# One attention kernel with expert layers: the sync queue's order written out, a half-size layout for the keys, and two stores of row sums instead of twelve

## The chip, the cores and the metric

The kernel runs on one core of one Trainium2 chip. The metric is device time in microseconds (us) from launch to end, the median of several runs. Engines are named as the profile names them: PE is the matrix engine, DVE the vector engine, ACT the scalar engine, POOL the GpSimd engine, and SP the sync engine, which here only issues transfers (DMAs). An engine works through its own instructions strictly in order; a DMA that SP issues must wait on SP for whatever its buffer or its source still needs, and everything behind it on SP waits too.

## The reference, cut to what matters

```python
# q, k, v: (8, 8, 576, 64), float32; batch B, heads H, positions S, width D
scores = scale * np.matmul(q, k.transpose(0, 1, 3, 2))
x = (psi_rel / psi_i)[..., None]              # from the positions alone
bias = np.maximum(x @ w1 + b1, 0.0) @ w2      # (S, S, H): one table per head
scores = scores + bias.transpose(2, 0, 1)[None]
attn = np.exp(scores - np.max(scores, axis=-1, keepdims=True))
attn = attn / (np.sum(attn, axis=-1, keepdims=True) + 1e-09)
out = np.matmul(attn, v)
x = out.transpose(0, 2, 1, 3).reshape(B * S, H * D)   # 4608 tokens x 512
return ((x @ moe_w1) * (x @ moe_w2) @ moe_w3) @ moe_w_out
```

The expert layers' weights arrive as 64-bit floats, which the kernel reads as pairs of 32-bit words and turns into 32-bit floats itself. The keys and queries come transposed, positions along the free dimension.

## The kernel before

**Three stages.** First a prologue computes the bias tables of all eight heads in 36 groups (`bias_group`): DVE and ACT make the hidden layer, PE multiplies, ACT scales the result into a tile `bev` (four buffers), and SP stores it to a table in device memory, `nb_d`. Then the attention runs, and last the expert layers in nine chunks of 512 tokens, three matmul passes to each product (lines 605 to 649), which read the attention's result from device memory and multiply it with the reciprocal row sums (`load_x`, `load_r`).

**Units.** The attention is worked through in 32 units, u = 0 to 31: four pairs of heads p, and in each the eight batches b. A unit has nine tiles of 128 rows: "0", "2", "4", "6" are head 0, "1", "3", "5", "7" head 1, and "M" the last 64 rows of both. For each tile PE multiplies queries with keys (`op_S`, line 259), DVE adds the bias and finds the row extreme (`op_T`, line 270, tile `ts`), ACT takes the exponential and, in the same instruction, the row sum (`op_E`, line 299), and DVE transposes pairs of tiles in 32 x 32 blocks (`op_R`, line 309, tile `pt`). One unit later PE multiplies the transposed block with v (`op_W`, line 352, eight parts W0 to W7), ACT copies the result out (`op_X`), and SP stores it (`op_x`, `x_d`). Every fourth unit DVE turns the collected sums into reciprocals (`op_r`, lines 316 to 319), and SP stores them to `r_m` and `r_t`.

**Transfers of a unit.** The steps l load q and k two units ahead, one tile per head (two buffers each, 288 KB a transfer), and v one unit ahead in four parts (one buffer each, 320 or 256 KB). `load_bias` loads the bias tables of a pair into two buffers per tile group: for pair 0 from the prologue's plan, for pair p + 1 from `op_T` in units b = 2 to 6 of pair p, one group a unit (576 KB, group M 288 KB). A queue of 24 weight pieces (`piece_of`, `narrow`) is converted beside the attention in units with b = 1 to 6: step c0 loads a piece's words (`wi`, 512 KB, two buffers), c1 and c2 are on ACT (lines 140 and 143; the first makes `wmag`), c3 and c7 on POOL (lines 146, 163, 164), c4 to c6 on DVE (lines 149, 155, 160).

**What sets the order.** `arrange` gives every step of every unit a planned time, in units of about a microsecond:

```python
PERIOD = 9 * L_T                                   # 12.87, a unit
at[f"lv{c}"] = -PERIOD + at[f"W{2 * c + 1}"][0] + 0.6, "SP"
at["c0"] = 0.2, "SP"
at["c1"] = t_of[1] + 1.6, "ACT"                    # 4.26
```

Worked out modulo the period, SP's steps stand at 0.2 (c0), 1.40 (v, last part), 2.50 (`op_x`), 4.50 (row sums), 6.36 and 6.46 (k and q of head 0, first part of v), 9.32 (v, second part), 11.31 and 11.41 (k and q of head 1, third part of v). The first tile's T stands at 2.00. `drive` sorts a plan by these times and emits the steps one by one. Inside `manual_schedule` the engines that are named keep the emitted order. SP is not among them: the order of its DMAs comes from the compiler's list scheduler, which lets a transfer go when, by its own estimate, buffer and data are ready. The plan is driven in several parts: steps at times below zero with the prologue, then the attention (line 506), then the fold and the expert layers. 

Of the kernel before, what the change touches and what calls it, by code (L numbers as in the profile page):

```python
# [9 lines left out]
F32 = mybir.dt.float32  # L10
# [8 lines left out]
P = 128  # L19
# [59 lines left out]
def relpos_attention_moe(  # L79
# [17 lines left out]
    nc = tc.nc  # L97
    NPAIR, B, _, S2 = q.shape
    S, D, H = S2 // 2, P // 2, 2 * NPAIR
# [5 lines left out]
    HS = S // 2  # L105
# [7 lines left out]
    dram = ctx.enter_context(tc.tile_pool(name="dram", bufs=1, space=DRAM))  # L113
# [52 lines left out]
        steps = [fetch, size, rest, clamp, shift, head, power, total]  # L166
        return steps if WIDE else [fetch] + [lambda: None] * 7

    def drive(plan):

        E_ = mybir.EngineType
        with tc.manual_schedule(engines={E_.PE, E_.Activation, E_.DVE, E_.Pool}):
            for _, _, step in sorted(plan, key=lambda e: e[:2]):
                step()

# [15 lines left out]
    nb_d = dram.tile([H, (S + 1) * NB_W], F32, name="nb_d")  # L191
    nb_v = nb_d[:, 0:S * NB_W].rearrange("h (i w) -> h i w", w=NB_W)[:, :, NB_L:NB_L + S]
    x_d = [dram.tile([P, NTOK], F32, name=f"x_d{p}") for p in range(NPAIR)]
    r_m = [dram.tile([2, B * 512], F32, name=f"r_m{p}") for p in range(NPAIR)]
    r_t = [dram.tile([2, B * 64], F32, name=f"r_t{p}") for p in range(NPAIR)]

# [1 line left out]
    raw = att_r.enter_context(tc.tile_pool(name="raw", bufs=2, side="right"))  # L200
# [6 lines left out]
    st = {u: {} for u in range(NU)}  # L207
# [27 lines left out]
    def op_l(u, which):  # L235
        p, b = units[u]
        n = int(which[1])
        if which[0] == "v":
            b0, b1 = VB[n]
            t = vp.tile([P, b1 - b0, 2, D], F32, name=f"v{n}")  # L240
            src = v[p, b].rearrange("p (b h d) -> p b h d", h=2, d=D)[:, b0:b1]
            for i in range(b0, b1):
                st[u]["v", i] = t[:, i - b0]
        else:
            t = st[u][which] = raw.tile([P, S], F32, name=which)
            src = {"q": q, "k": k}[which[0]][p, b][:, n * S:(n + 1) * S]
        nc.sync.dma_start(t, src)

    def op_S(u, t):

        d = st[u]
        s = d["s", t] = ps_s.tile([P, 2, 512], F32, name="s")
        for hf, rows in enumerate((lo, hi)):
            for g, outs in enumerate((lo, hi)):
                if t == "M":
                    h, q0 = g, 512
                else:
                    h, q0 = int(t) % 2, int(t) // 2 * P + 64 * g
                nc.tensor.matmul(  # L259
                    s[outs, hf, :HS], d[f"q{h}"][rows, q0:q0 + 64],  # L260
                    d[f"k{h}"][rows, hf * HS:(hf + 1) * HS], start=True, stop=True,
                )

    def op_T(u, t):
# [16 lines left out]
    for i in range(2):  # L281
        t = att.enter_context(tc.tile_pool(name=f"sums{i}", bufs=1)).tile([P, 64], F32, name=f"sums{i}")
# [28 lines left out]
    def op_r(u, n):  # L311
        if u % 4 < 3:
            return
        if n == "":
            r = SUMS[u // 4 % 2]
            nc.vector.tensor_scalar(r[:, 0:36], r[:, 0:36], 1e-9, None, op0=ALU.add)
            nc.vector.reciprocal(r[:, 0:36], r[:, 0:36])
            st[u]["rt"] = sm.tile([P, 64], F32, name="rt")
            nc.vector.transpose(st[u]["rt"], r)
            return  # L320
        p, b = units[u]
        rt, b0 = st[u]["rt"], b - 3
        for a in range(4):
            for h in range(2):
                o = r_m[p][h, b0 * 512:(b + 1) * 512].rearrange("(n a j) -> a n j", a=4, j=32)[a]
                nc.sync.dma_start(o, rt[32 * a + 16 * h:32 * a + 16 * h + 16, 0:32])
            o = r_t[p][a // 2, b0 * 64:(b + 1) * 64].rearrange("(b g j) -> g b j", g=2, j=32)[a % 2]
            nc.sync.dma_start(o, rt[32 * a:32 * a + 4, 32:64])

    def load_r(rb, p, rows, h, t0, t1):  # L330
        n = t0
        while n < t1:
            b, j = divmod(n, S)
            e = min(t1, b * S + (512 if j < 512 else S))
            src = r_m[p][h:h + 1, b * 512 + j:b * 512 + j + e - n] if j < 512 else \
                r_t[p][h:h + 1, b * 64 + j - 512:b * 64 + j - 512 + e - n]
            nc.sync.dma_start(rb[rows, n - t0:e - t0], src.broadcast_to([64, e - n]))
            n = e

    def op_W(u, n):  # L340
# [44 lines left out]
    def op_c(u, n):  # L385
        pieces[u][int(n)]()

    made = dict(l=op_l, S=op_S, T=op_T, E=op_E, R=op_R, r=op_r, W=op_W, X=op_X, x=op_x, c=op_c)
    later = []
    for (n, u), (at, on) in arrange(NU, pieces).items():  # L390
        step = lambda n=n, u=u: made[n[0]](u, n[1:])
        later.append((at, len(later), step, n, u))
    t_s = max(e[0] for e in later if e[3][0] in "SE") + 0.5
    end = max(e[0] for e in later) + 0.5
    later = [e[:3] for e in later]

    plan = [e for e in later if e[0] < 0.0]
    later = [e for e in later if e[0] >= 0.0]


    with ExitStack() as pro:
# [29 lines left out]
        def reach(G):  # L431

            return (G + 1) * GR - 1, S - 1 - G * GR
# [9 lines left out]
        for G in range(NGRP):  # L443
            n = max(reach(G)) + 1
            for vv in range(GV):
                e = min(busy, key=lambda e: busy[e] + COST[e][0] + COST[e][1] * n)
# [40 lines left out]
        for G in range(NGRP):  # L487
            at = -LEAD + G * PACE_B
            put(plan, bias_group(G), *(at + d for d in AT_BIAS))
            for ts in GROUPS:  # L490
                if G == (NGRP - 1 if ts == "M" else 8 * (int(ts[-1]) // 2) + 7):
                    plan.append((at + AT_BIAS[-1] + LAG_B, len(plan), lambda ts=ts: load_bias(0, ts)))
        drive(plan)


# [7 lines left out]

    PT = [pt.tile([P, 9, S], F32, name=f"pt{i}") for i in range(2)]

    drive([e for e in later if e[0] < t_s])
    later = [e for e in later if e[0] >= t_s]
    att_r.close()

# [74 lines left out]
    def load_x(c):  # L584
        for cc in range(NC):
            xr = xs.tile([P, CH], F32, name=f"xr{cc}", bufs=1)
            nc.sync.dma_start(xr, x_d[cc][:, c * CH:(c + 1) * CH])
            rb = xs.tile([P, CH], F32, name=f"rb{cc}", bufs=1)
            for h, rows in enumerate((lo, hi)):
                load_r(rb, cc, rows, h, c * CH, (c + 1) * CH)  # L590
            chunks[c]["x"][cc] = (xr, rb)
        yield
# [64 lines left out]
    for t in range(2):  # L657
        for m in range(2):
            put_w(later, w01, t, m, t_s + AT_W1 + PACE_W * (2 * t + m))
    drive([e for e in later if e[0] <= end])  # L660
    later = [e for e in later if e[0] > end]
    att.close()
# [3 lines left out]
    plan, t_f = [], t_s + AT_F + N_F * PACE_F0 + (2 * NF - N_F) * PACE_F + AT_FOLD[3]  # L666
# [77 lines left out]
```

## Time and profile before

| what | value |
|---|---|
| runs | 1175.22, 1181.52, 1184.53 us; median 1181.52 |
| profiled execution | 1180.03 us, its span 1178.2 us |
| PE / DVE / ACT / POOL busy | 1112.6 / 686.3 / 484.1 / 181.2 us |
| attention, first ts at | 65.7 us |
| expert layers' first `up` matmul on the chain at | 585.1 us |
| granted PE clock | 0.98 over the span |
| DMA traffic | 158.5 MB; share of the 16 engines 71% from 72 to 517 us, 13% after 700 us |

The profile's page gives busy time and shares for each engine, then groups of instructions: line, engine, operation, output<-input, count, then busy us, mean ns of one, and the idle time before them with what ended most of it. "issue" is idle time that ended though no semaphore was waited for. Rows of single instructions begin with the start and the duration in us; in brackets stand the idle time before and its releaser. The chain of waits is the path that ended last, followed back through whatever released each step. A row of a table by stretches gives the stretch, its length, the busy time of PE, PE's weight loads, DVE, ACT and POOL, the granted clock, the DMA share and GB/s. A row by DMA queue gives packets, MB and the share of 16 engines; q1 carries the kernel's data.

### The profile page before, as it was taken

The page shows a single profiled execution, that of the slowest core. Times are in us where ns is not written, and L with a number is a line of the kernel's source. Part 1 is how long each engine was busy: PE and PEld are TensorE (multiplying, and loading weights), DVE is VectorE, ACT ScalarE, POOL GpSimd, SP SyncE. Part 2 cuts the span into 40 slices and gives each one's busy share as a digit, 9 for nine tenths or more (in the row PEclk, how much of TensorE's full clock was granted, in tenths as well). Part 3 has the DMA queues.
Part 4 walks back from the last instruction along what each step waited for, and adds up shares of the span by engine and source line. Part 5 has one row for each costly group of instructions (what it writes and reads, how often), then busy time and mean ns, then how long its engine had stood idle before and what let it go on. Part 6 is the DMA issues. An engine that isn't in the chain of part 4 may idle for free.

```text
span 1178.2 us, 34156 instructions
## 1 busy us (share of the span) xinstructions
PE 1112.6 (94%) x14720; PEld 771.2 (65%) x14720; DVE 686.3 (58%) x1284; ACT 484.1 (41%) x1071; POOL 181.2 (15%) x152
## 2 busy tenths in 40 slices
PE   7769989998899999898999999999999999999998
PEld 3225445444444554466888888888888888888887
DVE  8779988998899999986885222223131222223111
ACT  6756655665566666664442212121211212121212
POOL 0003320321033123333543000000000000000000
PEclk9979999999999999998999999999999999999999
DMA  8887786767776766636431211202010211100000
GB/s 261 279 261 229 231 285 206 242 214 244 234 234 222 237 222 205 217 120 173 132 117 54 72 36 54 54 36 72 35 55 19 72 36 56 52 36 1 36 1 36
DMA packets 91959, 158.51 MB, mean 135 GB/s; under 512 B 18336, under 2 KB 32800, under 8 KB 91808
## 3 DMA queue, kind: packets, MB, share of 16 engines
q1 hardware_dynamic: 91376, 156.31, 41.6%
q8 instruction: 115, 1.88, 0.6%
q14 instruction: 36, 0.29, 0.1%
q10 hardware_dynamic: 432, 0.02, 0.0%
HBM read 126.36 MB, written 29.92 MB: 133 GB/s over the span
## 4 chain that ended last, share of the span: by engine, by line
PE 68%; DVE 19%; issue 5%; DMA 5%; ACT 2%; SPq 0%; DVEq 0%; POOL 0%; ACTq 0%; POOLq 0%
PE up L614 33%; PE o L639 17%; PE acc L352 8%; DVE ts L270 8%; DVE pt L309 7%; PE s L259 6%; PE wacc L573 3%; DMA nb_d<-bev 2%; DMA v<-in_v_dram 1%; PE bacc L473 1%; DVE wmag L155 1%; ACT pp L299 1%; DVE wi L160 1%; DVE zdve L459 1%; PE w3t L561 0%
## 5 line engine op out<-in xcount | busy, mean ns | idle before, releaser
L352 PE MATMUL acc<-pt,v 32*64 32x128 f32 (+1 forms) x9216 | 245.0, 298 | 21.9 <-issue 12.2
L352 PEld LDWEIGHTS acc<-pt,v 32*64 32x64 f32 x9216 | 158.2, 133 | 145.0 <-issue 110.7
L622 DVE TENSOR_TENSOR g<-up,a 128x512 f32<-128x512 f32 x72 | 49.8, 691 | 342.8 <-PE up L614 342.8
L299 ACT ACTIVATE pp<-ts,mx 128x576 f32<-128x576 f32 x256 | 196.5, 769 | 95.0 <-DVE mx L270 93.9
L259 PE MATMUL s<-k,q 64*64 64x288 f32 x2304 | 208.8, 442 | 21.2 <-DVE mx L270 16.0
L614 PE MATMUL up<-xl,wh 128*128 128x512 f32 x576 | 225.1, 391 | 0.0
L614 PE MATMUL up<-xh,wl 128*128 128x512 f32 x576 | 225.1, 391 | 0.0
L614 PE MATMUL up<-xh,wh 128*128 128x512 f32 x576 | 225.1, 391 | 0.0
L270 DVE CUSTOM_DVE_ANT_0 ts<-s,nb 128x576 f32<-128x576 f32 x256 | 184.9, 745 | 41.1 <-PE s L259 28.2
L639 PE MATMUL o<-w3s,gh 128*128 128x512 f32 x576 | 177.7, 390 | 0.0
L309 DVE STREAM_TRANSPOSE pt<-pp 128x1152 f32<-128x1152 f32 x128 | 175.5, 1371 | 0.1
L619 ACT COPY a<-up 128x512 f32<-128x512 f32 x72 | 42.3, 587 | 257.7 <-PE up L614 257.7
L259 PEld LDWEIGHTS s<-k,q 64*64 64x64 f32 x2304 | 63.3, 135 | 97.8 <-issue 48.1
L614 PEld LDWEIGHTS up<-xh,wl 128*128 128x128 f32 x576 | 108.2, 188 | 23.4
L614 PEld LDWEIGHTS up<-xl,wh 128*128 128x128 f32 x576 | 108.2, 188 | 23.4
L614 PEld LDWEIGHTS up<-xh,wh 128*128 128x128 f32 x576 | 108.2, 188 | 23.3
L639 PEld LDWEIGHTS o<-w3s,gh 128*128 128x128 f32 x576 | 108.1, 188 | 22.9
L625 ACT ACTIVATE gh<-g 128x512 fp32r<-128x512 f32 x72 | 45.5, 633 | 178.3 <-DVE g L622 178.3
L639 PE MATMUL o<-w3s,gl 128*128 128x512 f32 x288 | 112.1, 389 | 0.0
L600 POOL TENSOR_SCALAR xh<-xr 128x512 fp32r<-128x512 f32 x36 | 23.2, 645 | 443.3 <-DVE xr L596 443.3
L628 DVE TENSOR_TENSOR gl<-g,gh 128x512 fp32r<-128x512 f32 x72 | 51.6, 717 | 50.7 <-ACT gh L625 50.5
L146 POOL TENSOR_SCALAR wmag<-wmag 128x512 f32<-128x512 f32 x24 | 46.0, 1915 | 207.9 <-ACT wmag L140 174.0
(67 smaller groups left out, 937.3 us busy)
## 6 DMA issues: line engine op xcount, KB each, us to landing
v<-in_v_dram SPq DMA_DIRECT2D x64, 320.0 KB
k<-in_k_dram SPq DMA_DIRECT2D x64, 288.0 KB
q<-in_q_dram SPq DMA_DIRECT2D x64, 288.0 KB
v<-in_v_dram SPq DMA_DIRECT2D x64, 256.0 KB
wi<-in_moe_w_dram SPq DMA_DIRECT2D x32, 512.0 KB
nb_d<-bev SPq DMA_DIRECT2D x36, 295.5 KB
nb<-nb_d SPq DMA_DIRECT2D x16, 576.0 KB
x_d<-x SPq DMA_DIRECT2D x32, 288.0 KB
```

What stands on the lines that cost most here:

```text
L146: clamps.tensor_scalar(d["mag"], d["mag"], LEAST, MOST, op0=ALU.max, op1=ALU.min)
L259: nc.tensor.matmul(s[outs, hf, :HS], d[f"q{h}"][rows, q0:q0 + 64], d[f"k{h}"][rows, hf * HS:(hf + 1) * HS], start=True, stop=True,)
L270: nc.vector.tensor_tensor_reduce(out=halves(ts), in0=d.pop(("s", t))[:, :, :HS], in1=halves(NB[p, t]), op0=ALU.add, op1=ALU.min, scale=-1. ...
L299: nc.scalar.activation(d["p", ps][:, k * S:(k + 1) * S], ts, AF.Exp, bias=mx, scale=-1.0, accum_out=SUMS[u // 4 % 2][:, col:col + 1],)
L309: nc.vector.transpose(o, st[u].pop(("p", ts)))
L352: nc.tensor.matmul(acc[outs, a, c0:c0 + 32 * (t1 - t0)], d["v", b][rows, h], pt_[rows, t0:t1, 32 * b:32 * b + 32], start=(b == 0), stop=(b ...
L614: nc.tensor.matmul(acc, l[:, cc], r, start=(n == 0), stop=(n == 3 * NC - 1))
L619: nc.scalar.copy(a, ps[0])
L622: nc.vector.tensor_tensor(g, ps[1], a, op=ALU.mult)
L625: nc.scalar.activation(gh, g, AF.Copy)
L628: nc.vector.tensor_tensor(gl, g, f(gh), op=ALU.subtract)
L639: nc.tensor.matmul(d["o", t], l[:, sl], folded[ft][:, r], start=(ft == 0 and n == 0), stop=(ft == NF - 1 and n == 2),)
```

## The change

It has three parts.

1. SP joins the engines that keep the emitted order, in the attention's part of the plan only (line 506).
2. A key tile holds one head's 576 positions as 288 columns: positions 0 to 287 on partitions 0 to 63 and 288 to 575 on partitions 64 to 127. Before, both partition halves held all 576. The matmuls read the same rows; each transfer has 144 KB instead of 288. The host's layout of k follows.
3. The reciprocal row sums of four units go out in two transfers, one of [128, 32] to `r_m` and one of [128, 32] to `r_t`, instead of eight and four. Both destinations are laid out anew, and `load_r` reads `r_t` in two pieces of 32 positions.

```diff
-    def drive(plan):
+    def drive(plan, *more):
...
-        with tc.manual_schedule(engines={E_.PE, E_.Activation, E_.DVE, E_.Pool}):
+        with tc.manual_schedule(engines={E_.PE, E_.Activation, E_.DVE, E_.Pool, *more}):
...
-    r_m = [dram.tile([2, B * 512], F32, name=f"r_m{p}") for p in range(NPAIR)]
-    r_t = [dram.tile([2, B * 64], F32, name=f"r_t{p}") for p in range(NPAIR)]
+    r_m = [dram.tile([B // 4, 2, 4 * 512], F32, name=f"r_m{p}") for p in range(NPAIR)]
+    r_t = [dram.tile([B // 4, P, 32], F32, name=f"r_t{p}") for p in range(NPAIR)]
...
-            t = st[u][which] = raw.tile([P, S], F32, name=which)
-            src = {"q": q, "k": k}[which[0]][p, b][:, n * S:(n + 1) * S]
+            w = S if which[0] == "q" else HS
+            t = st[u][which] = raw.tile([P, w], F32, name=which)
+            src = {"q": q, "k": k}[which[0]][p, b][:, n * w:(n + 1) * w]
...
-                    d[f"k{h}"][rows, hf * HS:(hf + 1) * HS], start=True, stop=True,
+                    d[f"k{h}"][rows, :], start=True, stop=True,
...
-        rt, b0 = st[u]["rt"], b - 3
-        for a in range(4):
-            for h in range(2):
-                o = r_m[p][h, b0 * 512:(b + 1) * 512].rearrange("(n a j) -> a n j", a=4, j=32)[a]
-                nc.sync.dma_start(o, rt[32 * a + 16 * h:32 * a + 16 * h + 16, 0:32])
-            o = r_t[p][a // 2, b0 * 64:(b + 1) * 64].rearrange("(b g j) -> g b j", g=2, j=32)[a % 2]
-            nc.sync.dma_start(o, rt[32 * a:32 * a + 4, 32:64])
+        rt = st[u]["rt"]
+        o = r_m[p][b // 4].rearrange("h (n a j) -> a (h n) j", a=4, j=32)
+        nc.sync.dma_start(o, rt[:, 0:32])
+        nc.sync.dma_start(r_t[p][b // 4], rt[:, 32:64])
...
+                src = r_t[p][b // 4].rearrange("(h g b) j -> h b g j", h=2, g=2)[h:h + 1, b % 4].broadcast_to([64, 2, 32])
+                o = o.rearrange("p (g j) -> p g j", g=2)
...
-    drive([e for e in later if e[0] < t_s])
+    drive([e for e in later if e[0] < t_s], mybir.EngineType.SP)
```

More of the change, by code (lines that the diff above doesn't have):

```diff
@@ L334, in load_r @@
             e = min(t1, b * S + (512 if j < 512 else S))
-            src = r_m[p][h:h + 1, b * 512 + j:b * 512 + j + e - n] if j < 512 else \
-                r_t[p][h:h + 1, b * 64 + j - 512:b * 64 + j - 512 + e - n]
-            nc.sync.dma_start(rb[rows, n - t0:e - t0], src.broadcast_to([64, e - n]))
+            o = rb[rows, n - t0:e - t0]
+            if j < 512:
+                j += b % 4 * 512
+                src = r_m[p][b // 4, h:h + 1, j:j + e - n].broadcast_to([64, e - n])
+            else:
+                assert e - n == 64
+                src = r_t[p][b // 4].rearrange("(h g b) j -> h b g j", h=2, g=2)[h:h + 1, b % 4].broadcast_to([64, 2, 32])
+                o = o.rearrange("p (g j) -> p g j", g=2)
+            nc.sync.dma_start(o, src)
             n = e
@@ L712 @@
     pairs = heads // 2
-    for n in "qk":
-        a = inputs[n].reshape(-1, pairs, 2, seq, dim)
-        a = a.transpose(1, 0, 4, 2, 3)
-        inputs[n] = _np.concatenate([a, a], axis=2).reshape(pairs, -1, 2 * dim, 2 * seq)
+    a = inputs["q"].reshape(-1, pairs, 2, seq, dim).transpose(1, 0, 4, 2, 3)
+    inputs["q"] = _np.concatenate([a, a], axis=2).reshape(pairs, -1, 2 * dim, 2 * seq)
+    a = inputs["k"].reshape(-1, pairs, 2, 2, seq // 2, dim).transpose(1, 0, 3, 5, 2, 4)
+    inputs["k"] = a.reshape(pairs, -1, 2 * dim, seq)
     a = inputs["v"].reshape(-1, pairs, 2, seq // 32, 32, dim).transpose(1, 0, 4, 3, 2, 5)
```

## The prediction

> **What bounds the kernel now.** I read the page first, then the stretches of the attention stage, then the chain of waits, and last the queues and single instructions where the chain jumps.
>
> ```profile
> span 1178.2 us, 34156 instructions
> PE 1112.6 (94%) x14720; PEld 771.2 (65%) x14720; DVE 686.3 (58%) x1284; ACT 484.1 (41%) x1071; POOL 181.2 (15%) x152
> q8 instruction: 115, 1.88, 0.6%
> ...
> L352 PE MATMUL acc<-pt,v 32*64 32x128 f32 (+1 forms) x9216 | 245.0, 298 | 21.9 <-issue 12.2
> ```
> ```profile
> 159.46:192.69 33.23, 29.08 (x724) 15.07 (x720) 24.89 (x50) 16.59 (x42) 2.55 (x2) 0.90 0.72 229
> ...
> 278.38:310.47 32.09, 27.27 (x728) 14.45 (x728) 24.96 (x50) 16.59 (x42) 2.55 (x2) 0.95 0.82 258
> ```
>
> The busy 94% of PE is an average. After about 585 us the expert layers run on PE without a hole, and no edit touches PE work there. The attention stage (about 66 to 517 us, 32 units of one head pair and batch) is where the change acts. The chain of waits shows its pace:
>
> ```profile
> 204.58 1.29 DVE pt L309
> ...
> 217.77 1.29 DVE pt L309
> ```
>
> The same transpose comes 13.19 us later, and the chain between is DVE work: an undisturbed unit that carries a weight piece is bound by DVE at 13.19. Units 0 and 7 of each pair carry no piece; one of them lasts 12.56 (405.94 less 393.39 below). Units 4, 12, 20 and 28 add three DVE instructions of the row sums: unit 4, the first such, lasts 13.95 (132.37 less 118.42), 0.76 more.
>
> ```profile
> 78.52 0.72 DVE L270 CUSTOM_DVE_ANT_0 ts<-s,nb 128x576 f32<-128x576 f32 x1
> ...
> 118.42 0.75 DVE L270 CUSTOM_DVE_ANT_0 ts<-s,nb 128x576 f32<-128x576 f32 x1
> ...
> 132.37 0.74 DVE L270 CUSTOM_DVE_ANT_0 ts<-s,nb 128x576 f32<-128x576 f32 x1
> ...
> 393.39 0.74 DVE L270 CUSTOM_DVE_ANT_0 ts<-s,nb 128x576 f32<-128x576 f32 x1
> ...
> 405.94 0.72 DVE L270 CUSTOM_DVE_ANT_0 ts<-s,nb 128x576 f32<-128x576 f32 x1
> ...
> 502.67 0.75 DVE L270 CUSTOM_DVE_ANT_0 ts<-s,nb 128x576 f32<-128x576 f32 x1
> ```
>
> Units 1 to 30 begin at 78.52 and end at 502.67: 424.15 us. Their floor is 24 x 13.19 + 6 x 12.56 + 4 x 0.76 = 395.0. **So 29 us are lost, and that is what an edit of the transfers can win.** Units 7 and 8 (33.23 in the stretch above) and 15 and 16 (32.09) lose 15 of them against 2 x 12.56; the other 14 are spread.
>
> What are the holes? The worst end in "issue", in the middle of a group of matmuls, where no semaphore is waited for. The queues from 85 to 159 us, then from 159 to 166, then PE:
>
> ```profile
> q1 hardware_dynamic: 8049, 17.06, 71.0%
> q8 instruction: 16, 0.26, 1.4%
> ```
> ```profile
> q1 hardware_dynamic: 762, 1.85, 84.3%
> q14 instruction: 1, 0.01, 0.3%
> ```
> ```profile
> 166.64 0.48 PE L352 MATMUL acc<-pt,v 32*64 32x160 f32 x4
> 169.22 0.44 PE L352 MATMUL acc<-pt,v 32*64 32x160 f32 x10 [2.10 <-issue]
> ```
>
> 115 packets of 1.88 MB on q8 are 16 KB each, and 2 x 14720 PE instructions over 115 are 256 a packet: q8 brings PE its program. From 85 to 159 us it delivers 16 packets, one per 4.6 us. From 159 to 166 (second fence) not one starts while q1 holds 84% of the engines, and at 167.1 PE stops for 2.10 us. I read this as PE out of instructions, its fetch waiting behind data. The granted clock of 0.90 in that stretch adds slow matmuls after the hole. What filled q1 there:
>
> ```profile
> 161.40 0.39 SPq L229 DMA_DIRECT2D nb<-nb_d  x1
> ...
> 163.55 0.38 SPq L229 DMA_DIRECT2D nb<-nb_d  x1
> ...
> 168.99 0.38 SPq L229 DMA_DIRECT2D nb<-nb_d  x1
> ```
>
> The bias tables of the pair after next, 2.6 MB, go out as soon as units 7 and 15 free their buffers.
>
> **The change, part by part.**
>
> *Order, the bias tables.* In the written order load_bias is issued by op_T in units 2 to 6 of the pair before use, one table group a unit. The bunch at units 7-8 and 15-16 goes, and pair 1's tables leave 66 to 78 us. Cost: 576 KB more in 12 units and 288 KB in 3. Nobody waits for a table: it is needed at least two units later.
>
> *Keys.* 64 transfers of 288 KB become 144 KB. A unit with a piece moves 2816 KB instead of 3104 (k 2 x 288, q 2 x 288, v 1152, x_d 288, piece 512): 9% less. Matmuls read the same rows and counts: nothing on PE.
>
> Together I let 24 of the 29 us go: the 15 of the bunches nearly whole (0.5 stays), and of the scattered 14 about a third stays (4.5), since the load falls 9% where no table comes and rises 9% where one does, while the waits of the next paragraph give PE slack. Ends: 15 (the scattered ones stay) and 29.
>
> *Order, the weight piece.* This is the cost. Step c0 of a piece (its load wi) stands in the plan at 0.2, behind v2 (11.41 of the unit before) and ahead of v3; its user c1 (wmag on ACT) stands at 4.26. Before, the queue let wi go a whole unit ahead:
>
> ```profile
> 207.61 0.33 SPq L135 DMA_DIRECT2D wi<-in_moe_w_dram  x1
> ...
> 216.89 0.33 SPq L247 DMA_DIRECT2D k<-in_k_dram  x1
> ...
> 218.25 0.38 SPq L247 DMA_DIRECT2D v<-in_v_dram  x1
> ```
> ```profile
> 209.71 0.67 ACT L140 ACTIVATE wmag<-wi 128x512 f32<-128x512 f32 x1
> ...
> 211.03 0.77 ACT L299 ACTIVATE pp<-ts,mx 128x576 f32<-128x576 f32 x1
> ```
> ```profile
> 206.09 0.75 DVE L270 CUSTOM_DVE_ANT_0 ts<-s,nb 128x576 f32<-128x576 f32 x1
> ...
> 212.02 1.38 DVE L309 STREAM_TRANSPOSE pt<-pp 128x1152 f32<-128x1152 f32 x1
> ```
>
> This unit begins at 206.09. The wi of 207.61 is for the next unit, whose wmag comes some 15 us on. Afterwards wi follows v2, which waits for PE to free its buffer at 12.16 (218.25): wi leaves at about 12.6, 0.6 before the next unit. wmag is due at 3.62 of it (209.71). Behind wmag ACT has two exponentials, the second ending at 211.80, and DVE takes the transpose of their result at 212.02: 0.2 us of slack. A later wi stops ACT, then DVE, which has no reserve. wi lands behind k, q, v issued from 10.80 on: 144 + 288 + 320 + 512 = 1264 KB. Two bursts of the trace price that, from first issue to landing:
>
> ```profile
> 133.88 0.33 SPq L135 DMA_DIRECT2D wi<-in_moe_w_out_dram  x1
> ...
> 403.85 0.33 SPq L247 DMA_DIRECT2D k<-in_k_dram  x1
> ```
> ```profile
> 134.78 5.09 DMA x_d<-x
> ...
> 404.75 3.28 DMA v<-in_v_dram
> ```
>
> wi + v + x_d, 1056 KB, took 134.78 + 5.09 - 133.88 = 5.99 us; k + q + v, 896 KB, 4.18. In proportion, 1264 KB take 7.2 or 5.9, so wi lands 4.8 or 3.5 into the next unit, later than 3.62 + 0.2 by 1.0 or not at all. I take 0.6: the larger burst is the nearer one, but it ends in a store and has three loads on its heels. Of 24 pieces, 17 pay 0.6 (10); three (units 6, 14, 22) also have a bias table just ahead of wi, 2.3 us for 576 KB at the 258 GB/s of the second stretch, and pay 2.9 (9); in units 4, 12, 20, 28 the 0.76 of row-sum work on DVE covers most (1). **Sum +20; ends 6 and 29.**
>
> *Order, the prologue.* The first unit's v and two wi, hoisted into the prologue, now wait for the attention plan.
>
> ```profile
> 24.46 4.19 DMA nb_d<-bev
> 31.73 6.10 DMA nb_d<-bev
> ```
> ```profile
> 37.94 0.47 ACT L479 ACTIVATE bev<-bacc,post 128x256 f32<-128x256 f32 x1 [2.67 <-DMA nb_d<-bev]
> ```
> ```profile
> 57.45 0.31 ACT L479 ACTIVATE bev<-bacc,post 128x64 f32<-128x64 f32 x1 [1.32 <-DMA nb_d<-bev]
> ```
>
> The nb_d store behind the first wi took 1.9 us longer than the earlier one, and ACT waited for it; the second wait follows v and wi at 49 to 51 us. 1.9 + 1.3 can go: I take -3 (ends 0 and -4).
>
> *Row sums.* Ten issues fewer in each of eight bursts. They hold up the k and v behind them in every fourth unit, but these have most of a unit to spare: 0. Their order moves behind v3 and x_d, which wait for PE and ACT no longer than now: 0. load_r's 64 r_t loads in two pieces lie under the unbroken PE of the expert layers: 0; without that cover, 64 more small packets each.
>
> **Sum**, against the execution's own 1180.03 us (1178.2 of span and 1.8 around it; the median of the runs is 1181.52): 1180.03 - 24 - 3 + 20 = **1173**. After the fetch holes, what ends last is the wait for wi.
>
> Against the row of 2.10 us stands the Trainium skill, "Runtime: NRT & Kernel Launch", section "Instruction fetch mechanics": blocks of 16 KiB or 256 instructions, whose crossing is "mostly hidden". The block agrees with the 115 packets; the hiding does not, as the hole shows. By it the hole would have another cause, the 24 us would stay, and the sum would be 1197.
>
> **The rivals.**
> - *wi lands in time* (the 896 KB burst is the measure): only the three units behind a table pay 2. 1180 - 27 + 6 = **1159**. For it: less traffic than in either burst. Against: the other burst.
> - *wi is late by 1.6 on average*, the other side: 17 x 1.6 + 3 x 3.9 + 4 x 0.9 = 42.5, so 1180 - 27 + 42.5 = **1196**. Place: ACT's wmag, DVE's transpose behind it. Up to 0.95 a plain piece (16 + 10 + 1 = 27) it only eats the gain; beyond, the change is slower. Against: needs a landing at 5.4, over both bursts.
> - *Fetches do not wait for the backlog*: nothing of the 29 goes, 1180 - 3 + 20 = **1197**. Against: the 7 us without a q8 packet fall together with the bias loads.
> - *The order is not what binds*, the queue issues as now: the lighter keys alone take a third of the scattered 14 and 1 us of the bunches, 1180 - 6 = **1174**.
>
> By the Trainium skill, "DMA: Bandwidth & Descriptors", section "Queues, rings and completion order", an engine takes turns between queue rows packet by packet, so a fetch would wait for one packet, which is the third rival; the hole speaks against it, though no row shows the engine that carries q8.
>
> **How the numbers follow.** Chances: forecast 0.52 (1163 to 1183), wi in time 0.27, wi very late 0.09, no relief of fetches 0.07, order without effect 0.05. A measurement of this kernel tells about 1% from no change, so faster means below 1169.7: nearly all of the second case and a third of the first, 0.45. Slower (above 1193.3) are most of the third and fourth, 0.09; the rest is 0.46. The range 1155 to 1188 leaves out a fifth of the second case and most of the third and fourth, 0.19.
>
> **What would show it.** The first ts of the attention, now:
>
> ```profile
> 65.66 0.76 DVE L270 CUSTOM_DVE_ANT_0 ts<-s,nb 128x576 f32<-128x576 f32 x1 [11.41 <-DMA nb_d<-bev]
> ```
>
> In the profile after: ACT's wmag waiting for the DMA of wi, some 20 us in 24 times, and DVE's pt waiting for ACT in the same units (wrong if wmag never waits); one bias load in each of units 2 to 6; PE's "issue" holes down from 12.2 us to some 3, with none over 2; the first ts about 3 us before 65.66; the expert layers as long as now. The prediction fails most easily in the landing of wi, 0.6 us more or less a unit being 14 us in all.

## The result, and the profile after

The changed kernel takes 1209.91 us (median of four runs, 1203.86 to 1215.33) against 1180.2 us for the kernel before on the same chip: 1.0256 times as long, interval 1.0219 to 1.0294. It is slower by 30 us; the prediction was 1173 us. The profiled execution took 1208.99 us, its span 1207.2 us. Where one run of a kernel lay over 1.5% above its fastest (in e4, e5 and e9 below), the ratio leaves that slow run out, while the median and the range include it.

The page of the changed kernel first, with the rows that answer to those shown of before (line 259 is now 260, 270 is 271, 299 is 300, 309 is 310, 352 is 356):

```profile
span 1207.2 us, 34040 instructions
PE 1127.3 (93%) x14720; PEld 778.1 (64%) x14720; DVE 688.9 (57%) x1284; ACT 486.1 (40%) x1071; POOL 181.5 (15%) x152
...
q8 instruction: 115, 1.88, 0.6%
...
L260 PE MATMUL s<-k,q 64*64 64x288 f32 x2304 | 216.6, 457 | 51.2 <-DVE mx L271 47.7
L356 PE MATMUL acc<-pt,v 32*64 32x128 f32 (+1 forms) x9216 | 251.3, 307 | 11.8 <-DVE pt L310 8.7
...
L310 DVE STREAM_TRANSPOSE pt<-pp 128x1152 f32<-128x1152 f32 x128 | 175.6, 1372 | 37.6 <-ACT pp L300 37.5
```

The "issue" holes of PE that led the second matmul row before (12.2 us) are down to 2.1. A new idle time stands on the transpose: 37.5 us of DVE waiting for ACT, where the kernel before had 0.1 of any kind. The lists of waits of DVE, ACT and PE (waiter, releaser, total us, times, longest) name the chain behind it:

```profile
DVE pt L310 <- ACT pp L300: 37.5, 21, 4.6
DVE ts L271 <- PE s L260: 27.0, 29, 1.8
```
```profile
ACT wmag L140 <- DMA wi<-in_moe_w_dram: 32.9, 19, 4.5
...
ACT wmag L140 <- DMA wi<-in_moe_w_out_dram: 15.6, 8, 3.5
```
```profile
PE acc L356 <- issue: 2.1, 4, 0.8
...
PE s L260 <- issue: 0.8, 2, 0.6
```

ACT waits for the weight words `wi`, DVE for ACT. In the kernel before, the first of DVE's two waits isn't in the list. The second was about as long as now, but most of it (some 20 us) lay in units 7, 8 and 13 to 16, where the fetch holes were:

```profile
DVE ts L270 <- PE s L259: 28.9, 26, 3.4
```

Now the stretches (length; busy time of PE, its weight loads, DVE, ACT, POOL; granted clock; DMA share; GB/s): units 1 to 30, the two places where the bias tables used to bunch (units 7-8 and 15-16), and all that follows the first ts of unit 31. The last fence is the kernel before.

```profile
72.12:531.81 459.69, 406.29 (x10772) 213.31 (x10768) 396.19 (x785) 274.43 (x675) 104.73 (x70) 0.94 0.63 201
...
531.81:1207.20 675.39, 664.85 (x3520) 542.37 (x3512) 235.94 (x352) 162.05 (x287) 75.90 (x74) 0.99 0.19 59
```
```profile
171.48:197.44 25.96, 24.98 (x724) 13.32 (x720) 24.67 (x50) 16.70 (x42) 2.57 (x2) 1.00 0.59 185
292.56:319.08 26.52, 25.70 (x748) 13.73 (x736) 24.77 (x50) 16.70 (x42) 2.55 (x2) 1.00 0.61 184
```
```profile
502.67:1178.20 675.53, 665.07 (x3520) 542.65 (x3512) 234.19 (x352) 162.16 (x287) 75.64 (x74) 0.99 0.19 59
```

The expert layers are as long as before (675.39 against 675.53). The bunches are gone: 33.23 became 25.96, 32.09 became 26.52. And yet units 1 to 30 take 459.69 instead of 424.15, 64.7 over the floor of 395.0. The two waits of DVE, 37.5 and 27.0, make nearly all of it (up to 2 us of the second lie in units 0 and 31).

Why two waits? Unit 5 (134.34 to 152.33) as single rows, then its granted clock:

```profile
131.93 0.33 SPq L248 DMA_DIRECT2D k<-in_k_dram  x1
...
132.70 0.33 SPq L248 DMA_DIRECT2D v<-in_v_dram  x1
...
133.08 0.42 SPq L248 DMA_DIRECT2D q<-in_q_dram  x1
...
133.60 0.61 SPq L135 DMA_DIRECT2D wi<-in_moe_w_out_dram  x1
...
140.98 0.68 ACT L140 ACTIVATE wmag<-wi 128x512 f32<-128x512 f32 x1 [2.94 <-DMA wi<-in_moe_w_out_dram]
...
143.21 1.38 DVE L310 STREAM_TRANSPOSE pt<-pp 128x1152 f32<-128x1152 f32 x1 [2.87 <-ACT pp L300]
...
145.63 1.24 PE L260 MATMUL s<-k,q 64*64 64x288 f32 x8 [2.51 <-DVE mx L271]
...
150.05 0.76 DVE L271 CUSTOM_DVE_ANT_0 ts<-s,nb 128x576 f32<-128x576 f32 x1 [1.85 <-PE s L260]
```
```profile
139.00:143.00 4.00, 3.82 (x112) 1.81 (x96) 1.34 (x3) 2.02 (x5) 1.25 (x1) 1.00 0.69 230
143.00:147.00 4.00, 1.49 (x21) 0.51 (x24) 3.79 (x8) 2.82 (x8) 0.66 (x1) 0.75 0.23 70
147.00:150.00 3.00, 3.00 (x64) 1.70 (x67) 1.20 (x3) 1.17 (x4) 0.00 (x0) 0.50 0.03 5
150.00:153.00 3.00, 3.00 (x76) 1.67 (x75) 2.95 (x5) 0.87 (x2) 0.45 (x1) 0.70 0.37 94
```

`wi` leaves 0.74 before the unit (133.60 against 134.34), as predicted (0.6), but reaches ACT 6.6 into it, not about 4.4. DVE loses 2.87. PE, which waits for DVE's scores, stands still for 2.51, and after that it runs at a granted clock of 0.50 for about 6 us: eight matmuls take 1.24 us there. Now PE is the late one, and DVE waits for it once more, 1.85. The unit lasts 18.0 instead of 13.2. Unit 26 has a shorter wait (0.79 on DVE) and PE stands still for 1.25:

```profile
471.25 0.71 PE L260 MATMUL s<-k,q 64*64 64x288 f32 x8 [1.25 <-DVE mx L271]
```

Here eight matmuls take 0.71 at once, nothing follows, and the unit lasts 14.07. In the changed kernel every unit whose transpose waits 1.5 us or more pays a second time (1.27 to 1.85 each in 11 units, 17.4 in all); those with 1.49 and less don't (at most 0.6).

### The profile page after: what moved, and what is told of

Read it like the earlier page. It is cut to its first block, busy times and chain, and to the rows that moved or that the text cites. A ratio compares the mean times of both kernels' runs of the same rounds, so it can differ in the third digit from the quotient of the medians.

```text
span 1207.2 us, 34040 instructions
## 1 busy us (share of the span) xinstructions
PE 1127.3 (93%) x14720; PEld 778.1 (64%) x14720; DVE 688.9 (57%) x1284; ACT 486.1 (40%) x1071; POOL 181.5 (15%) x152
## 3 DMA queue, kind: packets, MB, share of 16 engines
q8 instruction: 115, 1.88, 0.6%
## 4 chain that ended last, share of the span: by engine, by line
PE 67%; DMA 13%; DVE 9%; issue 5%; ACT 4%; SPq 2%; POOL 0%; DVEq 0%; ACTq 0%; POOLq 0%
PE up L618 33%; PE o L643 16%; PE acc L356 7%; DMA wi<-in_moe_w_dram 7%; PE s L260 6%; DMA wi<-in_moe_w_out_dram 4%; ACT pp L300 3%; DVE pt L310 3%; DVE ts L271 3%; PE wacc L577 3%; PE bacc L477 2%; SPq L248 2%; DMA nb_d<-bev 1%; DVE zdve L463 0%; PE w3t L565 0%
## 5 line engine op out<-in xcount | busy, mean ns | idle before, releaser
L260 PE MATMUL s<-k,q 64*64 64x288 f32 x2304 | 216.6, 457 | 51.2 <-DVE mx L271 47.7
L356 PE MATMUL acc<-pt,v 32*64 32x128 f32 (+1 forms) x9216 | 251.3, 307 | 11.8 <-DVE pt L310 8.7
L356 PEld LDWEIGHTS acc<-pt,v 32*64 32x64 f32 x9216 | 163.5, 137 | 140.4 <-issue 100.0
L310 DVE STREAM_TRANSPOSE pt<-pp 128x1152 f32<-128x1152 f32 x128 | 175.6, 1372 | 37.6 <-ACT pp L300 37.5
```

Source lines behind the costliest of these rows:

```text
L260: nc.tensor.matmul(s[outs, hf, :HS], d[f"q{h}"][rows, q0:q0 + 64], d[f"k{h}"][rows, :], start=True, stop=True,)
L310: nc.vector.transpose(o, st[u].pop(("p", ts)))
L356: nc.tensor.matmul(acc[outs, a, c0:c0 + 32 * (t1 - t0)], d["v", b][rows, h], pt_[rows, t0:t1, 32 * b:32 * b + 32], start=(b == 0), stop=(b ...
```

## The experiments

Each ratio is against the kernel before, run on the same chip beside the kernel in question. Its medians there were 1180.2 to 1182.3 us, so that times of different kernels are also compared directly.

**e1_no_order.** The changed kernel, SP's order given back to the compiler.

```diff
-    drive([e for e in later if e[0] < t_s], mybir.EngineType.SP)
+    drive([e for e in later if e[0] < t_s])
```

> The changed kernel with the sync queue's order left to the scheduler again; the half-size keys and the two stores of row sums stay. Theory (the weight piece's load wi, ordered behind v2 and q, lands after ACT wants it): wi goes a unit ahead again, ACT's wmag waits for no DMA in the attention, 1170 to 1180 us. Rival (the new key layout or the new stores slow the transfers): stays at 1200 or more.

Measured: 1171.09 us, 0.9901 (0.9863 to 0.994). The half-size keys and two stores alone bring about 11 us; the order is what costs. ACT's wmag waits for no `wi` in the attention, as expected. Units 7 and 8 last 33.22 again:

```profile
156.73:189.95 33.22, 29.47 (x724) 15.44 (x720) 24.89 (x51) 16.59 (x42) 2.56 (x2) 0.90 0.81 244
```

**e3_order_only.** The kernel before with only the order fixed (the diff of e1 turned round; full-size keys, twelve stores).

> The kernel before with the sync queue's order fixed in the attention and nothing else: full-size keys, twelve stores. Theory: wi is late as in the changed kernel, and later by the 144 KB more of k ahead of it; 1208 to 1225 us. Rival (keys or stores are the cause): 1180 or less.

Measured: 1232.38 us, 1.0393 (1.0314 to 1.0472), a little over what was expected. With more traffic both waits grow:

```profile
DVE pt L309 <- ACT pp L299: 47.5, 23, 3.9
DVE ts L270 <- PE s L259: 35.1, 40, 1.8
```

**e2_piece_early.** The changed kernel, the load of the piece planned 10.87 earlier. In the profile it leaves 11.6 to 13.5 us before its unit begins (the first one earlier still).

```diff
-    at["c0"] = 0.2, "SP"
+    at["c0"] = 2.2 - PERIOD, "SP"
```

> The changed kernel with one number moved: c0 at 2.2 of the unit before instead of 0.2 of its own, so that wi is ordered a good 10 us earlier; the order stays fixed. Theory: the 38 us in which DVE waits for ACT go, and with them the 20 us or so of slow matmuls behind the holes on PE; 1145 to 1158 us. Rival (the fixed order harms through other transfers that stand behind a waiting one, v or q): no more than 10 us are won, 1197 or more.

Measured: 1157.43 us (1157.24 to 1157.8), 0.9785 (0.9749 to 0.9821): 52 us below the changed kernel by one planned time, and faster than both kernels. The wait of pt for ACT is gone from the list, and with it most of the second wait:

```profile
DVE ts L271 <- PE s L260: 11.3, 21, 0.9
```
```profile
73.72:479.70 405.98, 384.67 (x10768) 202.68 (x10768) 394.34 (x785) 272.57 (x675) 104.68 (x70) 1.00 0.73 226
```

Units 1 to 30 take 405.98, 11.0 over the floor. **So the late piece costs 64.7 - 11.0 = 53.7 us in the changed kernel: 37.5 of waiting, and 16 more behind it.**

**e4_q_before_v.** In the plan, q of a head and a part of v have the same time (6.46 and 11.41), and the changed kernel issues v first. v2 waits for PE (its buffer), q1 behind it, `wi` behind q1. Here q goes ahead of v.

```diff
-            at[f"l{n}{h}"] = -2 * PERIOD + s_of[4 + 4 * h] + 0.8 + 0.1 * k, "SP"
+            at[f"l{n}{h}"] = -2 * PERIOD + s_of[4 + 4 * h] + 0.8 + 0.05 * k, "SP"
```

> The changed kernel with q planned 0.05 earlier, so that q comes ahead of v in the queue and not behind the wait of v for PE (in the changed kernel the two stand at the same planned time, and v came first). Theory: q is through earlier, wi lands about 0.5 us earlier in 24 units, and fewer holes are long enough to slow PE's clock; 1185 to 1198 us. If wi's own place is all that counts: 1203 to 1210.

Measured: 1191.29 us, 1.0072 (1.004 to 1.0104). The first wait falls by 8.9, the second by 13.8:

```profile
DVE pt L310 <- ACT pp L300: 28.6, 21, 4.1
...
DVE ts L271 <- PE s L260: 13.2, 17, 1.9
```

**e10_early_q_before_v.** The same move in the kernel with the early piece.

> The kernel with the early weight piece and half keys (1157.4), with q0 and q1 planned 0.05 earlier so that they leave ahead of v0 and v2. If that move helped the changed kernel (1191 against 1210) only through wi, it does nothing here: 1155 to 1159. If q itself was late behind v (PE's scores waiting for q), it gains here too: 1145 to 1152.

Measured: 1161.1 us, 0.9828 (0.98 to 0.9856), not better than e2's 1157.43 and slightly over the expected band of the first case. PE's "issue" holes are 7.0 us here against 4.6 in e2, with single ones of up to 1.6. What e4 won, it won through `wi`.

**e5_tables_bunched.** The changed kernel; the five table groups of the next pair leave together at the end of unit 6.

```diff
-        if b == 2 + GROUPS.index(GROUP[t]) and p + 1 < NPAIR and done.issuperset(GROUP[t]):
-            load_bias(p + 1, GROUP[t])
+        if b == 6 and t == "7" and p + 1 < NPAIR:
+            for g in GROUPS:
+                load_bias(p + 1, g)
```

> The changed kernel with one move: the five table groups of the next pair go out together at the end of unit 6 of a pair, instead of one a unit in units 2 to 6, so none of them flies beside a weight piece. Theory A (wi lands late because the tables share the engines with it): wi takes about 5.2 us in all pairs, as in pair 3 now, instead of 6.3 in units 2 to 6, and DVE's pt waits for ACT fall from 37.5 to 15 to 22 us. Theory B (the tables have nothing to do with it, the wait of the queue for v2 and q1 alone is to blame): the landing and the 37.5 stay. Theory C (the program's fetches wait behind a bunch of data): holes of PE ending in 'issue' come back at the ends of the first three pairs, 4 to 8 us a bunch. A and C together: 37.5 - 18 less, its follow-up of some 12 less, 12 to 24 more, so 1192 to 1204; A without C 1178 to 1186; B with C 1222 to 1235.

Measured: 1202.37 us (1190.91 to 1215.56), 1.0155 (1.0087 to 1.0223); the profiled execution is the shortest of these, 1190.91. In it `wi` takes 5.4 us in units 2 to 6 of the first three pairs (6.4 before the move), pt's waits fall to 20.7, and the holes come back:

```profile
DVE pt L311 <- ACT pp L301: 20.7, 20, 1.9
```
```profile
173.04 1.36 PE L357 MATMUL acc<-pt,v 32*64 32x128 f32 x29 [2.34 <-issue]
```

Theory A holds fully for units 6, 14 and 22, where a table left directly ahead of `wi` (waits of 11.4 together, now 1.7). For units 2 to 5 of those pairs 17.9 became 11.7, but this can't all be the tables' doing: in six of these twelve (3, 5, 11, 13, 19 and 21) no table was under way beside `wi` in the changed kernel, and they held 9.2 of the 17.9. What else stretches `wi` there is open; two flights of the changed kernel, unit 5 and unit 29, differ in the rate at which the engines deliver:

```profile
133.60:140.91 7.31, 6.97 (x176) 3.21 (x159) 6.74 (x14) 2.66 (x9) 2.56 (x2) 1.00 0.85 262
503.48:507.94 4.46, 4.29 (x128) 2.17 (x111) 4.46 (x10) 2.73 (x9) 2.55 (x2) 1.00 0.95 335
```

**e6_early_bunched.** The same bunch in the kernel with the early piece, where no piece can be late.

> The kernel with the early weight piece (1157), and the tables bunched in the same way. No weight piece can be late here, so the bunch is alone. Theory C (program fetches wait behind a bunch of data): PE holes ending in 'issue' of over 1 us come back at units 7-8, 15-16 and 23-24, 4 to 8 us each time with the slow clock behind them: 1167 to 1180. Rival (a fetch waits for no more than a packet of data, the holes had another cause): no such hole, 1155 to 1159.

Measured: 1164.28 us, 0.9869 (0.9829 to 0.9909), 7 above e2 and 3 below the expected band. The holes are there (the profiled execution, 1167.87 us, is the longest of the four). PE, then the queues from 164 to 171 us:

```profile
163.49 0.79 PE L357 MATMUL acc<-pt,v 32*64 32x128 f32 x29 [1.08 <-issue]
...
170.61 1.23 PE L260 MATMUL s<-k,q 64*64 64x288 f32 x6 [2.65 <-issue]
```
```profile
q1 hardware_dynamic: 1305, 2.37, 100.7%
q8 instruction: 1, 0.02, 0.9%
```

With q1 full, one 16 KB packet of program arrives in 7 us, and PE stops twice with nothing to wait for. No row shows the fetch itself; that PE runs dry is read from the holes coming and going with the bunch. Units 7-8 and 23-24 lose 7.0 and 6.0 against e2; units 15-16 only 1.5, which is why the sum is small.

**e7_act_077 and e8_act_308.** Does a long first wait bring the second one? These leave every transfer alone and add one, or four, activations to ACT ahead of wmag in the 24 units with a piece (n is 1 or 4; the added work serves nothing else), in the kernel with the early piece.

```diff
     def op_c(u, n):
+        if n == "1":
+            for _ in range(1):        # 4 in e8
+                nc.scalar.activation(junk, junk, AF.Copy)
         pieces[u][int(n)]()
```

> The kernel with the early weight piece (1157), with one more activation of 128x576 (some 0.77 us) on ACT ahead of wmag in each of the 24 units with a piece; no transfer is touched. DVE's transpose becomes late by 0.77 less the slack of 0.2. Theory D (a short hole costs its own length): 24 x 0.57 = 14 more, 1168 to 1173, granted clock as before. Theory E (any wait of DVE for ACT costs more than itself): 1180 or above.

> The same with four such activations (3.1 us) in each of the 24 units. DVE late by 2.9 a unit. If a wait costs its own length: 24 x 2.9 = 70 more, about 1227, clock as before. Theory D (a PE hole of over about 1.6 us is followed by some 3.4 us at half clock, by which PE's scores come late once more, 1.3 to 1.8 us a unit): 31 to 43 more still, 1258 to 1270, with DVE's ts waiting for PE's s some 24 times and the mean granted clock down to about 0.95.

Measured: e7 1166.19 us, 0.9877 (0.9829 to 0.9925); e8 1242.61 us, 1.0528 (1.0488 to 1.0567). The DVE waits of e7, then of e8:

```profile
DVE ts L271 <- PE s L260: 8.6, 16, 1.0
DVE pt L310 <- ACT pp L300: 8.6, 19, 0.6
```
```profile
DVE pt L310 <- ACT pp L300: 57.6, 24, 2.8
DVE ts L271 <- PE s L260: 37.2, 39, 1.8
```

The short wait costs itself: 8.6 of waiting, 8.8 us more than e2, and the other wait does not grow (8.6 against 11.3). The long one does not: 57.6 of waiting, 85 us more, the other wait 26 longer, in 18 more places. Both times lie below the bands given for Theory D (an added activation took 0.67 us, not 0.77, and the waits are 0.4 and 2.4 a unit, not 0.57 and 2.9), but e8 lies above the linear 1227. Two units side by side, unit 5 of e7 and of e8:

```profile
138.96 0.71 PE L260 MATMUL s<-k,q 64*64 64x288 f32 x8 [0.84 <-DVE mx L271]
```
```profile
150.75 1.24 PE L260 MATMUL s<-k,q 64*64 64x288 f32 x8 [2.98 <-DVE mx L271]
```
```profile
130.15:143.81 13.66, 12.66 (x368) 6.66 (x360) 13.28 (x27) 9.79 (x24) 4.47 (x3) 1.00 0.72 214
```
```profile
139.80:157.06 17.26, 14.12 (x368) 7.44 (x360) 13.28 (x28) 11.93 (x27) 4.47 (x3) 0.90 0.54 169
```

After 0.84 us of standing still PE goes on at full clock; after 2.98 the same eight matmuls take 1.24.

Is it the hole itself or the clock behind it that brings the second wait? Unit 29 of e8 tells them apart. Its transpose waits 2.52 us and PE stands still for 2.98, both as in unit 5, but the granted clock stays at 1.00:

```profile
544.73 0.71 PE L260 MATMUL s<-k,q 64*64 64x288 f32 x8 [2.98 <-DVE mx L271]
```
```profile
533.77:549.57 15.80, 12.66 (x368) 6.65 (x360) 13.28 (x27) 11.82 (x27) 4.47 (x3) 1.00 0.59 184
```

There is no second wait in it, and it is shorter than unit 5 by 1.46 us. That is the second wait of unit 5:

```profile
154.78 0.76 DVE L271 CUSTOM_DVE_ANT_0 ts<-s,nb 128x576 f32<-128x576 f32 x1 [1.46 <-PE s L260]
```

So the second wait comes from the half clock behind the hole. Of the 22 units of e8 whose transpose waited over 1.5 us, 21 had a stretch of half clock, and 20 of these had a second wait, of 0.85 to 1.85. In all runs, 14 units had a transpose wait of 1.2 us or more and kept the full clock, and none of them had a second wait of over 0.21.

**e9_order_early_old_keys.** The kernel before with the written order and the early piece, but its own keys and stores.

> The kernel before with the written order of SP and the early weight piece (c0 at 2.2 of the unit before), but with its own full-size keys and twelve stores. Theory F (the lighter keys matter mostly through the landing of a late wi; with an early piece they save only fetch waits): 3 to 9 us above the 1157.4 of the same kernel with half keys, 1160 to 1167. Theory G (the lighter keys are worth as much as between the changed kernel and the one with the order alone, some 22 us, by the load on the engines itself): 1175 to 1182.

Measured: 1172.94 us (1169.98 to 1192.83), 0.9926 (0.9906 to 0.9946). So lighter keys and two stores are worth 15.5 us here, between both theories: more than F allowed. Part of it may be fetch waits, 12.4 us of "issue" holes against 4.6 in e2:

```profile
PE acc L352 <- issue: 10.8, 13, 1.7
...
PE s L259 <- issue: 1.6, 2, 1.1
```

Keys and stores were only tried together, so which of them it is stays open.

## Why the prediction was wrong, step by step

- **The bound and the floor: right.** DVE's floor of 395.0 stood; e2 comes within 11.0 of it with the same work. It is a little low: units 8, 16 and 24 were put at 12.56 and took 13.4 or more in every run.
- **Bias tables and keys, -24: right in mechanism, 6 too large.** PE's "issue" holes fell to 2.9 us with none over 0.85 (predicted: some 3, none over 2), and e6 brought them back by bunching the tables alone. Cleared of the late piece (e2), the loss of 29.2 falls to 11.0: -18. Within the step, the keys may have been sized too small: the rival "keys alone" gave 6 us; e1 and e9 showed 11 and 15.5 for keys and stores together.
- **"Order, the weight piece", +20: this step failed. It cost 53.7.** Its mechanism was right at every link: issue 0.7 ahead of the unit, wmag waiting for `wi` (41.7 us in 21 of the 24 units; the lists above hold waits of the expert layers' own weights too), pt waiting for ACT. Three sizes in it were not. For the waits, 20 was predicted as 10 for 17 plain pieces, 9 for the three behind a table and 1 for the four units with row sums; measured were 23.5, 11.4 and 2.7, the 37.5 in all. The other 16 stand behind the waits.
  - *The plain pieces.* 0.6 each was nearly right where no tables fly: the six pieces of the last pair wait 4.7 together, 0.78 each. In units 2 to 5 of the other pairs the mean is 1.5. The estimate scaled one burst by its bytes; it had no term for the rate, which was 262 and 335 GB/s in the two flights shown under e5. That q1 would go behind v2 and directly ahead of `wi` was in the plan as a tie of planned times, and was not looked at; e4 prices it at about 19 us.
  - *The three behind a table.* 2.9 predicted; 3.64, 3.16 and 4.58 measured.
  - *What follows a long wait.* The sum counted a wait at its own length. In the changed kernel, from about 1.5 us up, PE's clock falls to half behind it, and DVE waits again: some 16 us that no term held. e7 and e8 show it with no transfer touched.
- **Prologue, -3: right in mechanism, too small.** 5.8 was measured (first ts at 59.86 instead of 65.66), beyond the stated end of -4. ACT's waits for the nb_d stores fell from 9.2 to 2.5 us. In other runs with the written order the first ts came between 59.5 and 63.1.
- **Expert layers unchanged: right.** Row sums at 0 were not tried by themselves.

With the measured terms the sum closes: 1180.0 - 18.2 - 5.8 + 53.7 = 1209.7 against 1208.99. As the terms come from these same traces, this shows only that nothing outside them moved. The rival on the other side (1196) asked for 1.6 a piece; the pieces came to 37.5 / 24 = 1.56 on average, and it still fell 13 short, since it had no term for the half clock. Its chance of 0.09 leant on two bursts of a trace in whose attention no `wi` was ever waited for, and on a sum in which each wait cost no more than itself.

## What to carry to other kernels

When an order is written down for a queue, go through every transfer that the free order had let run ahead, and give each at least the longest landing seen under load, not the middling one: here one planned time moved the same change from 1.0256 to 0.9785. Price a wait on the engine that feeds PE by the length of PE's hole: here a short hole cost itself, and one of two microseconds and more mostly cost another 0.85 to 1.85 us, by the half clock behind it. The kernel in which the transfer ended on the critical path also scattered more (1203.9 to 1215.3 us over four runs, against 1157.2 to 1157.8 with the transfer early); why was not tried.

## What the hardware showed that was not expected

PE's granted clock fell to 0.50 after a hole of 2.51 us and stayed there for about 6 us, with PE busy all the time; after 1.25 us it did not fall. The length alone does not decide: a hole of 1.88 us (unit 10 of the changed kernel) left it at 1.00 and one of 1.84 (unit 18) was followed by 0.50, and 2.98 us did either in e8. What else does is open. The Trainium skill, "TensorE: Matmul & The Clock Gate", Part 1, puts the fall to half rate behind an idle window of about 3.4 us. The half rate agrees; holes of 1.84 and 2.51 us were enough here.

PE stands still, for want of its program by this reading, while data fill the engines: 2.65 us with one fetch in 7 us (e6), and none over 0.85 when the same tables go out one at a time (the changed kernel and e2; with q ahead of v, in e4 and e10, single holes reach 1.7).
